# Two pairs of items in one stretch of 64x64 matmuls, masked scores in the place of k's columns

## The chip, the cores and the metric

The kernel runs on one core of one Trainium2 chip. The metric is the device time of one execution in microseconds (us), the median of several runs. The engines' names are those of the profile: PE (TensorE matmul), PEld (its weight loads), DVE (VectorE), ACT (ScalarE), POOL (GpSimd), SP (SyncE, which issues the DMAs).

## The reference

Retention (attention with a decay in place of the softmax) over 8 batches x 8 heads, sequence 576, head size 64, and behind it a feed-forward layer of 512 -> 2048 -> 512 on 4608 tokens, all in float32:

```python
scores = (q @ k.T) / sqrt(64)            # per batch and head
Dmat   = where(i >= j, gamma[h] ** (i - j), 0)
ret    = (scores * Dmat) @ v
x      = ret, heads side by side          # (4608, 512)
h      = x @ w_in                         # (4608, 2048)
out    = (h - tanh(h)) @ w_out            # (4608, 512)
```

## The kernel before, in words

The sequence is cut into 9 blocks of 64 positions (`C = 64`, `NC = 9`). A block holds 8 batches x 64 positions = 512 tokens (`BLK`). Retention goes block by block with a state per batch and head: a block's output is q times the state so far, plus the masked scores of the block itself times v; then k's rows times v are added to the state. An *item* is one batch in one block (8 heads, as 2 x 4 matrices of 64x64), a *pair* is two items; pair p belongs to block p // 4, and there are 36 (`NP`).

**Feed-forward.** Weights and x are split into a high and a low word, and three products are added. `mm1(n, f)` (L327) makes column block f of h for block n in 12 matmuls of 128x512 into one PSUM bank, `mm2(n, f)` (L393) multiplies the activated h of f by w_out in 12 matmuls into the four banks o0 to o3. Between them `activate` runs ACT tanh (L353), DVE subtraction (L354), ACT cast to the high word gh (L355), DVE subtraction to the low word gl (L356). `store` copies the four o banks at the end of a block (ACT L410, DVE L412) and stores them (L414).

**Retention.** All 64x64 matmuls have line L252 (`run`). `m_score` makes the scores of an item, `m_state` what is to be added to the state, `m_out` the output (`own`): first state times q, then v times masked scores. `run` lays two of the first list and two of the second side by side, so that the four quadrants of the array are used. `entry(p, sc)` is one *stretch*: scores of pair p + 1, states and outputs of pair p; behind it DVE masks the scores (L263, into the buffer pm), ACT and DVE split the output into xh and xl (L278, L280), and DVE adds to the state (L311). The trace shows each 64x64 matmul twice.

**PSUM has eight banks:** o0 to o3, two called h, one called new, one called own. mm1 takes the h banks in turn, and so do the scores of a stretch (`s`); the new states have `new` for themselves, and the outputs `own`.

**Order.** Every engine works its instructions in exactly the order in which the program writes them (`in_order`); semaphores are set by the framework from what reads and writes which tile.
- First part (`seq`, to about 125 us): block 0's items, then mm1 of blocks 0 and 1, while ACT and DVE convert the weights (`guard`, `unit`: L95 to L124). Results of mm1 that are needed later are spilled to DRAM.
- Second part (`late`, 32 steps k): mm2 of block 1 and then of block 0; spilled h are fetched (L363), activated (`resume`, `words`: L368 to L376). At k = 3, 8, 13 and 18 stands one stretch, for pairs 8 to 11.
- Third part: blocks n = 2 to 8. For each f: mm1(n, f), then mm2 of the f before. While block n is worked on, the items of block n + 1 get their retention: at f = 1, 5, 9 and 13 a stretch stands between mm1(n, f) and mm2(n, f - 1). Block 8 has none.

**Loads.** A pair's q, k (columns), v and k (rows) are one tile `a` of 1 MB, two buffers. Behind each stretch `load_pair(p + 2)` is issued on SP (L171) and POOL scales q and v (`prep`, L185, L186); the table for q changes with the block (L161).

Of the kernel before, what the change touches and what calls it, by code (L numbers as in the profile page):

```python
# [9 lines left out]
F32 = mybir.dt.float32  # L10
# [12 lines left out]
C = 64  # L23
# [8 lines left out]
WARM = 26  # L32

# [34 lines left out]
def retention_ffn(ctx: ExitStack, tc: tile.TileContext, ins, out, spill):  # L68
# [10 lines left out]


# [10 lines left out]
    def guard(t, f, begin=False):  # L91

        if (t, f) not in masks:
            masks[t, f] = pool.tile([P, DM], I32, tag="cv", bufs=3, name=f"m{t}{f}")
            nc.scalar.activation(masks[t, f], wraw[t, f][:, :, 1].bitcast(F32), AF.Tanh, scale=STEP)  # L95
            if begin:
                return
# [32 lines left out]
    last, going, pace = [], [], []  # L130
# [22 lines left out]
    loaded, scored, xs, qtabs = {}, {}, {}, {}  # L153
# [9 lines left out]
    def load_pair(p, u=None):  # L163

        if p >= NP:
            return
        c, pr = divmod(p, B // 2)
        load_qtab(c)
        a = loaded["pair", p] if u == 1 else pool.tile([P, 2, 4, 4, C], F32, tag="a", name=f"a{p}")
        if u is None:  # L170
            nc.sync.dma_start(a, qkv_d[c - 1, 2 * pr : 2 * pr + 2].rearrange("u p t i s -> p u t i s"))  # L171
        else:
            nc.sync.dma_start(a[:, u], qkv_d[c - 1, 2 * pr + u])
        loaded[2 * p], loaded[2 * p + 1] = a[:, 0], a[:, 1]
        loaded["pair", p] = a
        loaded["qv", p] = a[:, :, 0], a[:, :, 2]

    def prep(p, q=True):
# [3 lines left out]
        a = loaded["pair", p]  # L182
        if q:
            table = qtabs[c].unsqueeze(1).broadcast_to([P, 2, 4, C])
            nc.gpsimd.tensor_tensor(a[:, :, 0], a[:, :, 0], table, op=ALU.mult)  # L185
        nc.gpsimd.tensor_tensor(  # L186
            a[:, :, 2], a[:, :, 2], vtab[:, c].unsqueeze(1).unsqueeze(3).broadcast_to([P, 2, 4, D]), op=ALU.mult
        )
# [3 lines left out]
    def load_early(p):  # L192
        c, pr = divmod(p, B // 2)
        if pr < 2:
            return load_pair(p)
        src = qkv_d[c - 1, 2 * pr : 2 * pr + 2].rearrange("u p t i s -> p u t i s")
        parts = []
        for t in range(2):
            parts.append(const.tile([P, 2, 2, 4, C], F32, tag=f"wo{2 * (pr - 2) + t}", name=f"a_early{p}_{t}"))
            nc.sync.dma_start(parts[t], src[:, :, 2 * t : 2 * t + 2])  # L200
            behind(tc, pace[-1])
        for u in range(2):
            loaded[2 * p + u] = Parts([part[:, u] for part in parts])
        loaded["qv", p] = parts[0][:, :, 0], parts[1][:, :, 0]

    def scale_q(p):
        q, table = loaded["qv", p][0], qtabs[p // (B // 2)]
        nc.vector.tensor_tensor(q, q, table.unsqueeze(1).broadcast_to([P, 2, 4, C]), op=ALU.mult)

    def scale_v(p):  # L210
        v = loaded["qv", p][1]
# [43 lines left out]
    def after_score(j, sc, n):  # L255
# [5 lines left out]
        else:  # L261
            pm = pool.tile([P, 2, 4, C], F32, tag="pm", bufs=1, name=f"pm{j}")
            nc.vector.tensor_tensor(  # L263
                pm[:, :n].rearrange("p u i q -> p (u i) q"), sc.rearrange("p u i q -> p (u i) q"),
                mask.unsqueeze(1).broadcast_to([P, 4 * n, C]), op=ALU.mult,
# [22 lines left out]

    def entry(p, sc, more=None):
        c0, pr = divmod(p, B // 2)  # L290
        new = psp.tile([P, 2, 4, D], F32, tag="new", bufs=1, name=f"new{p}")
        o = psp.tile([P, 2, 4, C], F32, tag="own", bufs=1, name=f"own{p}")
        same, other = [], []
        for u in range(2):
            if p + 1 < NP:
                same += m_score(2 * p + 2 + u, sc[:, u])
            other += m_out(2 * p + u, o[:, u])
        if c0 < NC - 1:
            for u in range(2):
                same += m_state(2 * p + u, new[:, u])  # L300
# [3 lines left out]
        if p + 1 < NP:  # L304
            after_score(2 * p + 2, sc, 2)
# [3 lines left out]
        if c0 < NC - 1:  # L309
            st = state[:, 2 * pr : 2 * pr + 2]  # L310
            nc.vector.tensor_tensor(st, new, st, op=ALU.add)  # L311
# [342 lines left out]
```

## Time and profile before

| | |
|---|---|
| median of 3 runs | 890.01 us (889.89 to 890.73) |
| profiled execution | 891.8 us, span 890.0 us, mean granted PE clock 0.995 |
| PE busy | 877.6 us, 99% of the span |
| PEld / DVE / ACT / POOL busy | 724.3 / 363.3 / 287.7 / 67.7 us |
| 64x64 matmuls and their weight loads | L252 |
| stretches from block 2's items on | 28 |

A row of the timeline gives start and duration in us, engine, line, operation, output <- inputs, shape, and in brackets how long the engine stood idle before it and what released it. Rows of the chain are start, duration and what ran. A matmul's end is modelled, so PE's pace is read from the spacing of the starts. In a table by windows stand for each stretch of time the busy us of PE, PEld, DVE, ACT and POOL, then the granted PE clock, the share of the DMA engines and GB/s.

### The profile page before, as it was taken

The page shows a single profiled execution, that of the slowest core. Times are in us where ns is not written, and L with a number is a line of the kernel's source. Part 1 is how long each engine was busy: PE and PEld are TensorE (multiplying, and loading weights), DVE is VectorE, ACT ScalarE, POOL GpSimd, SP SyncE. Part 2 cuts the span into 40 slices and gives each one's busy share as a digit, 9 for nine tenths or more (in the row PEclk, how much of TensorE's full clock was granted, in tenths as well). Part 3 has the DMA queues.
Part 4 walks back from the last instruction along what each step waited for, and adds up shares of the span by engine and source line. Part 5 has one row for each costly group of instructions (what it writes and reads, how often), then busy time and mean ns, then how long its engine had stood idle before and what let it go on. Part 6 is the DMA issues. An engine that isn't in the chain of part 4 may idle for free.

```text
span 890.0 us, 17595 instructions
## 1 busy us (share of the span) xinstructions
PE 877.6 (99%) x7848; PEld 724.3 (81%) x7848; DVE 363.3 (41%) x548; ACT 287.7 (32%) x503; POOL 67.7 (8%) x59
## 2 busy tenths in 40 slices
PE   7999999999999999999999999999999999999997
PEld 6777878788888888888888888888888888888886
DVE  6879777653432332333233233323323322222222
ACT  4887774443222222222222222222222221222222
POOL 0001001210111110111111111111000111000000
PEclk8999999999999999999999999999999999999999
DMA  9966965551311131102111131113111201002001
GB/s 354 325 231 212 342 193 171 167 167 48 96 54 49 48 96 49 54 30 68 47 54 49 49 95 54 49 48 96 49 54 47 62 35 48 1 1 49 1 1 47
DMA packets 31372, 82.06 MB, mean 92 GB/s; under 512 B 3776, under 2 KB 4928, under 8 KB 31296
## 3 DMA queue, kind: packets, MB, share of 16 engines
q1 hardware_dynamic: 30768, 80.02, 27.8%
q8 instruction: 61, 1.00, 0.5%
q10 hardware_dynamic: 528, 0.92, 0.3%
q14 instruction: 15, 0.12, 0.0%
HBM read 63.62 MB, written 17.30 MB: 91 GB/s over the span
## 4 chain that ended last, share of the span: by engine, by line
PE 90%; DMA 3%; DVE 3%; ACT 2%; issue 0%; SPq 0%; DVEq 0%
PE o L393 44%; PE h L327 38%; PE s L252 3%; DMA rwo<-in_w_out_dram 2%; PE new L252 2%; PE own L252 2%; DMA rwi<-in_w_in_dram 1%; DVE mo L110 0%; DVE mo L112 0%; ACT mi L95 0%; ACT mi L98 0%; PE new_first L252 0%; DVE mi L105 0%; DVE wi L124 0%; ACT wi L117 0%
## 5 line engine op out<-in xcount | busy, mean ns | idle before, releaser
L327 PE MATMUL h<-xh,wi 128*128 128x512 f32 x1152 | 307.0, 392 | 2.7 <-ACT g L339 0.8
L393 PE MATMUL o<-wo,gh 128*128 128x512 f32 x1144 | 291.6, 393 | 0.4 <-DVE ob L412 0.4
L327 PEld LDWEIGHTS h<-xh,wi 128*128 128x128 f32 x1152 | 216.3, 189 | 49.7 <-ACT g L339 1.3
L393 PEld LDWEIGHTS o<-wo,gh 128*128 128x128 f32 x1144 | 212.3, 188 | 46.8 <-DVE ob L412 1.5
L354 DVE TENSOR_TENSOR g<-h,g 128x512 f32<-128x512 f32 x114 | 78.8, 691 | 367.1 <-ACT g L353 367.1
L353 ACT ACTIVATE g<-h 128x512 f32<-128x512 f32 x114 | 68.3, 599 | 420.9 <-PE h L327 420.1
L393 PE MATMUL o<-wo,gl 128*128 128x512 f32 x572 | 157.3, 389 | 0.0
L327 PE MATMUL h<-xl,wi 128*128 128x512 f32 x576 | 154.5, 390 | 0.0
L327 PEld LDWEIGHTS h<-xl,wi 128*128 128x128 f32 x576 | 108.7, 189 | 22.9
L393 PEld LDWEIGHTS o<-wo,gl 128*128 128x128 f32 x572 | 107.4, 188 | 22.3
L356 DVE TENSOR_TENSOR gl<-g,gh 128x512 fp32r<-128x512 f32 x113 | 81.0, 717 | 77.5 <-ACT gh L355 70.0
L355 ACT CAST gh<-g 128x512 fp32r<-128x512 f32 x113 | 70.1, 620 | 86.2 <-DVE g L354 86.2
L185 POOL TENSOR_TENSOR a<-a,qtab 128x512 f32<-128x512 f32 x27 | 36.3, 1344 | 605.7 <-DMA a<-in_qkv_dram 547.3
L252 PE MATMUL own<-a,state 64*64 64x64 f32 x960 | 58.9, 221 | 0.0
L252 PE MATMUL own<-pm,a 64*64 64x64 f32 x960 | 57.5, 218 | 0.0
L252 PEld LDWEIGHTS own<-a,state 64*64 64x64 f32 x960 | 47.8, 134 | 0.4 <-issue 0.4
L252 PEld LDWEIGHTS own<-pm,a 64*64 64x64 f32 x960 | 48.0, 135 | 0.0
L252 PEld LDWEIGHTS s<-a 64*64 64x64 f32 x960 | 30.3, 134 | 10.6 <-issue 10.2
L186 POOL TENSOR_TENSOR a<-a,vtab 128x512 f32<-128x512 f32 x28 | 32.2, 1152 | 67.4 <-DVE mi L112 67.4
L252 PE MATMUL s<-a 64*64 64x64 f32 x960 | 34.4, 221 | 0.0
L376 DVE TENSOR_TENSOR gl<-s,gh 128x512 fp32r<-128x512 f32 x30 | 21.6, 720 | 31.2 <-PE o L393 24.4
L375 ACT CAST gh<-s 128x512 fp32r<-128x512 f32 x30 | 18.6, 621 | 39.0 <-PE o L393 27.4
(67 smaller groups left out, 465.0 us busy)
## 6 DMA issues: line engine op xcount, KB each, us to landing
a<-in_qkv_dram SPq DMA_DIRECT2D x29, 1024.0 KB, 5.2
out_dram<-ob SPq DMA_DIRECT2D x69, 128.0 KB, 2.4
rwi<-in_w_in_dram SPq DMA_DIRECT2D x16, 512.0 KB, 5.8
rwo<-in_w_out_dram SPq DMA_DIRECT2D x16, 512.0 KB, 5.1
s<-spill_dram SPq DMA_DIRECT2D x30, 256.0 KB, 2.7
spill_dram<-g SPq DMA_DIRECT2D x20, 256.0 KB, 5.2
a<-in_first_dram SPq DMA_DIRECT2D x7, 384.0 KB, 5.0
spill_dram<-home SPq DMA_DIRECT2D x10, 256.0 KB, 6.3
```

What stands on the lines that cost most here:

```text
L185: nc.gpsimd.tensor_tensor(a[:, :, 0], a[:, :, 0], table, op=ALU.mult)
L186: nc.gpsimd.tensor_tensor(a[:, :, 2], a[:, :, 2], vtab[:, c].unsqueeze(1).unsqueeze(3).broadcast_to([P, 2, 4, D]), op=ALU.mult)
L252: nc.tensor.matmul(out_, w, x, start=start, stop=stop)
L327: nc.tensor.matmul(hp, win[f][:, a, cc, :], x[:, cc, :], start=(k == 0), stop=(k == 3 * NCC - 1))
L353: nc.scalar.activation(g, h, AF.Tanh)
L354: nc.vector.tensor_tensor(g, h, g, op=ALU.subtract)
L355: nc.scalar.copy(gh, g)
L356: nc.vector.tensor_tensor(gl, g, gh.bitcast(F32), op=ALU.subtract)
L375: nc.scalar.copy(gh, g)
L376: nc.vector.tensor_tensor(gl, g, gh.bitcast(F32), op=ALU.subtract)
L393: nc.tensor.matmul(ops[n][t], g[:, t * P : (t + 1) * P], wout[f_][:, a, :], start=(f_ == first and k == 0), stop=(f_ == final and k == 2),)
```

## The change

From pair 8 on, two stretches become one of two *halves*. `entry2(p)` does pairs p and p + 1: first half scores of p + 1, states and outputs of p; then, with no full-size matmul between, states of p + 1, scores of p + 2, outputs of p + 1. The states no longer have the bank `new`: scores and states of both halves take the two h banks in turn, and the second half's outputs go into `new`.

```diff
+    def entry2(p):
+        more, states = p + 2 < NP, p // (B // 2) < NC - 1
+        sc, o = bank(f"s{p + 1}", "h"), bank(f"own{p}", "own")
+        same = pair(m_score, p + 1, sc)
+        if states:
+            new = bank(f"new{p}", "h")
+            same += pair(m_state, p, new)
+        run(same, pair(m_out, p, o))
+        for u in range(2):
+            after_score(2 * p + 2 + u, sc[:, u : u + 1], 1)
+        if states:
+            add_state(p, new)
+        low = after_out(2 * p, o, 2, False)
+        o, same = bank(f"own{p + 1}", "new"), []
+        if states:
+            new = bank(f"new{p + 1}", "h")
+            same += pair(m_state, p + 1, new)
+        if more:
+            sc = bank(f"s{p + 2}", "h")
+            same += pair(m_score, p + 2, sc)
+        run(same, pair(m_out, p + 1, o))
+        if states:
+            add_state(p + 1, new)
+        low()
+        if more:
+            after_score(2 * p + 4, sc, 2)
+        after_out(2 * p + 2, o, 2)
+        for q, t in ((p + 2, 1), (p + 3, 1), (p + 3, 0), (p + 4, 0)):
+            load_part(q, t)
+            prep(q, t)
...
+    def add_state(p, new):
+        st = state[:, 2 * (p % (B // 2)) : 2 * (p % (B // 2)) + 2]
+        nc.vector.tensor_tensor(st, new, st, op=ALU.add)
```

The stretches stand at other places: in the second part at k = 4 and 14, in blocks 2 to 7 at f = 3 and 11 and behind mm2, so that mm1 of the next f follows.

```diff
-        if k in (3, 8, 13, 18):
-            entry(p, psp.tile([P, 2, 4, C], F32, tag="h", bufs=2, name=f"s{n}_{f}"))
-            p += 1
+        if k in (4, 14):
+            entry2(p)
+            p += 2
...
             mm1(n, f)
-            if n + 1 < NC and f % 4 == 1:
-
-                sc = psp.tile([P, 2, 4, C], F32, tag="h", bufs=2, name=f"s{n}_{f}")
-                entry((n + 1) * B // 2 + f // 4, sc)
             todo.append((n, f))
             if (n, f) != (NC - 1, NF - 2):
                 mm2(*todo.pop(0))
+            if n + 1 < NC and f in (3, 11):
+
+                entry2((n + 1) * B // 2 + f // 8 * 2)
```

A pair is loaded as two tiles of 512 KB, `qk` (q and k's columns, three buffers) and `vr` (v and k's rows, two), and pm is gone: the masked scores are written over k's columns.

```diff
-            pm = pool.tile([P, 2, 4, C], F32, tag="pm", bufs=1, name=f"pm{j}")
+            u = j % 2
+            pm = parts[j // 2, 0][:, u : u + n, 1]
...
+        if k == 18:
+            load_part(B + 2, 0)
```

The small buffers of the first two parts (masks of the weights, spilled h, tanh, output copies) get places with fixed numbers instead of two rings: for the output copies

```diff
-            ob = pool.tile([P, DM], F32, tag="cv", bufs=3, name=f"ob{n}_{t}")
+            ob = place(2 + t % 3, f"ob{n}_{t}")
```

How the order on the engines changes, at three places. *First, the stretch in block 6.* PE, the end of a stretch before (`a` is the pair, `new` the states, `own` the output, `o_0` and `o_1` the banks of mm2):

```order
L252 MATMUL new_6014<-a_5661 64x64 x2
L252 MATMUL own_6015<-a_5661,state 64x64 x2
L252 MATMUL new_6014<-a_5661 64x64 x2
L252 MATMUL own_6015<-pm_5860,a_5661 64x64 x2
L393 MATMUL o_0_6091<-wo_1214,gh_0_5959 128x512 [waits Activation_49]
L393 MATMUL o_1_6092<-wo_1214,gh_0_5959 128x512 [waits DVE_49]
```

PE now, the end of a merged stretch (`qk` and `vr` are the pair's two tiles):

```order
L265 MATMUL s_6194<-qk_5840 64x64 x2
L265 MATMUL own_6192<-qk_5837,state 64x64 x2
L265 MATMUL s_6194<-qk_5840 64x64 x2
L265 MATMUL own_6192<-qk_5837,vr_5834 64x64 x2
L368 MATMUL h_4_6278<-xh_5343,wi_432 128x512 [waits DVE_49]
L368 MATMUL h_4_6278<-xh_5343,wi_432 128x512 x3
```

Instead of mm2, mm1 follows (`h_4`), in the h bank that held the second half's states, and it waits for DVE. On DVE, the work of a stretch before:

```order
L354 TENSOR_TENSOR g_1_6006<-h_1_5993,g_1_6006 128x512 [waits Activation_49]
L356 TENSOR_TENSOR gl_1_6008<-g_1_6006,gh_1_6007 128x512 [waits Activation_49]
L263 TENSOR_TENSOR pm_6080<-s_1_6013,mask 128x512 [waits PE_49]
L280 TENSOR_TENSOR xl_6083<-own_6015,xh_6082 128x2x4x64 [waits Activation_49]
L311 TENSOR_TENSOR state<-new_6014,state 128x512
L354 TENSOR_TENSOR g_2_6120<-h_2_6107,g_2_6120 128x512 [waits Activation_49]
```

DVE now, for a merged stretch:

```order
L400 TENSOR_TENSOR gl_3_6102<-g_3_6100,gh_3_6101 128x512 [waits PE_49,Activation_49]
L278 TENSOR_TENSOR qk_5837<-s_6119,mask 128x256 [waits DMAHW3_49,PE_49,Pool_49]
L278 TENSOR_TENSOR qk_5837<-s_6119,mask 128x256
L308 TENSOR_TENSOR state<-new_6121,state 128x512 [waits PE_49]
L308 TENSOR_TENSOR state<-new_6193,state 128x512 [waits PE_49]
L295 TENSOR_TENSOR xl_6190<-own_6120,xh_6189 128x2x4x64 [waits Activation_49]
L278 TENSOR_TENSOR qk_5840<-s_6194,mask 128x2x256 [waits DMAHW4_49,PE_49,Pool_49]
L294 TENSOR_TENSOR xl_6190<-own_6192,xh_6189 128x2x4x64 [waits Activation_49]
```

The first masks are two pieces with one wait between them, for the last of the scores; each state addition has a wait of its own for PE. *Second, DVE at the first stretch of the second part.* Before (k = 3; `mo` and `wo` are a weight being converted, gl_2, s_3 and s_4 the h that are activated):

```order
L376 TENSOR_TENSOR gl_2_1681<-s_2_1605,gh_2_1680 128x512 [waits PE_49,Activation_49]
L369 TENSOR_TENSOR s_3_1636<-s_3_1636,th_3_1684 128x512 [waits DMAHW1_49,Activation_49]
L124 TENSOR_TENSOR wo_1666<-mo_1609,wo_1666 128x512 [waits DVE_49]
L263 TENSOR_TENSOR pm_1757<-s_1_1690,mask 128x512 [waits PE_49]
L280 TENSOR_TENSOR xl_1760<-own_1692,xh_1759 128x2x4x64 [waits Activation_49]
```

And now (k = 4):

```order
L420 TENSOR_TENSOR gl_2_1677<-s_2_1602,gh_2_1676 128x512 [waits PE_49,Activation_49]
L413 TENSOR_TENSOR s_3_1632<-s_3_1632,th_3_1680 128x512 [waits DMAHW5_49,Activation_49]
L137 TENSOR_TENSOR wo_1662<-spare,wo_1662 128x512 [waits DVE_49]
L420 TENSOR_TENSOR gl_3_1699<-s_3_1632,gh_3_1698 128x512 [waits PE_49,Activation_49]
L413 TENSOR_TENSOR s_4_1658<-s_4_1658,th_4_1702 128x512 [waits DMAHW6_49,Activation_49]
L278 TENSOR_TENSOR qk_1162<-s_1707,mask 128x256 [waits PE_49]
L278 TENSOR_TENSOR qk_1162<-s_1707,mask 128x256
```

Two more operations stand ahead of the masks. *Third, PE at the start of a block.* Before, mm1(6, 1) and behind it the stretch:

```order
L327 MATMUL h_1_5993<-xl_5243,wi_350 128x512 x4
L327 MATMUL h_1_5993<-xh_5242,wi_350 128x512 x4
L252 MATMUL s_1_6013<-a_5865 64x64 [waits DMAHW4_49,DVE_49,Pool_49]
L252 MATMUL s_1_6013<-a_5865 64x64
L252 MATMUL own_6015<-a_5661,state 64x64 [waits PE_49]
```

And now, mm1(6, 1) and behind it mm2(6, 0):

```order
L368 MATMUL h_1_6019<-xh_5343,wi_354 128x512 x4
L437 MATMUL o_0_6039<-wo_1216,gh_0_5985 128x512 [waits Activation_49]
L437 MATMUL o_1_6040<-wo_1216,gh_0_5985 128x512 [waits DVE_49]
L437 MATMUL o_2_6041<-wo_1216,gh_0_5985 128x512 [waits Activation_49]
L437 MATMUL o_3_6042<-wo_1216,gh_0_5985 128x512 [waits DVE_49]
```

The four output copies of the block before, which these waits are for, no longer have a stretch's time.

More of the change, by code (lines that the diff above doesn't have):

```diff
@@ L32 @@
 WARM = 26
+LATE = 22
 NP = NC * B // 2
@@ L93, in guard @@
         if (t, f) not in masks:
[L94 removed]
+            k = stream.index((t, f))
+            if k < LATE:
+                masks[t, f] = place(k % 3, f"m{t}{f}", I32)
+            else:
+                if not spare:
+                    spare.append(pool.tile([P, 4, DM], I32, tag="xl", name="spare"))
+                masks[t, f] = spare[0][:, k % 4]
             nc.scalar.activation(masks[t, f], wraw[t, f][:, :, 1].bitcast(F32), AF.Tanh, scale=STEP)
@@ L167, in load_pair, with prep @@
         c, pr = divmod(p, B // 2)
[L168 to L178, printed above, removed]
+        if t == 0:
+            load_qtab(c)
+        if (p, t) not in parts:
+            tag = ("qk", "vr")[t]
+            parts[p, t] = pool.tile([P, 2, 2, 4, C], F32, tag=tag, bufs=3 - t, name=f"{tag}{p}")
+            for u in range(2):
+                loaded.setdefault(2 * p + u, Parts([None, None])).parts[t] = parts[p, t][:, u]
+        src = qkv_d[c - 1, 2 * pr : 2 * pr + 2].rearrange("u p t i s -> p u t i s")
+        queue.dma_start(parts[p, t][:, at], src[:, at, 2 * t : 2 * t + 2])
+    def load_pair(p):
+        for t in range(2):
+            load_part(p, t)
+    def prep(p, t):
         if p >= NP:
@@ L287, in first_states, with bank, pair @@
         return ms, lambda: nc.scalar.copy(state[:, b : b + 2], new)
-    def entry(p, sc, more=None):
[L290 to L300, printed above, removed]
+    def bank(name, tag):
+        return psp.tile([P, 2, 4, D], F32, tag=tag, bufs=2 if tag == "h" else 1, name=name)
+    def add_state(p, new):
+        st = state[:, 2 * (p % (B // 2)) : 2 * (p % (B // 2)) + 2]
+        nc.vector.tensor_tensor(st, new, st, op=ALU.add)
+    def pair(what, p, bank):
+        return what(2 * p, bank[:, 0]) + what(2 * p + 1, bank[:, 1])
+    def entry(p, sc, more=None):
+        new, o = bank(f"new{p}", "new"), bank(f"own{p}", "own")
+        same, other = pair(m_score, p + 1, sc) + pair(m_state, p, new), pair(m_out, p, o)
         if more is not None:
```

72 lines of the change are left out of this document (34 added, 38 removed).

## The prediction

> **What bounds the kernel now.** I read the page first (busy times, then the chain that ended last), then the chain in order of time, then one 64x64 stretch on the timeline, and then the four places at which the change sets a new neighbour beside TensorE.
>
> ```profile
> PE 877.6 (99%) x7848; PEld 724.3 (81%) x7848; DVE 363.3 (41%) x548; ACT 287.7 (32%) x503; POOL 67.7 (8%) x59
> PE 90%; DMA 3%; DVE 3%; ACT 2%; issue 0%; SPq 0%; DVEq 0%
> ```
>
> PE is the bound: 99% of the span, 90% of the chain. What PE does not have to wait for costs nothing; every wait that is added to it is added to the time. VectorE is at 41%, so its work is cheap, but its *lateness* at one place is not.
>
> ```profile
> 493.23 2.95 PE o L393 x12
> 496.18 2.72 PE h L327 x12
> 517.24 2.95 PE o L393 x12
> ```
>
> The chain gives the size of a block's pieces: 12 full matmuls are 2.72 us (0.2267 each), and one stretch comes every 517.24 - 493.23 = 24.01 us. Eight pieces of 2.72 are 21.76, so a stretch costs 24.01 - 21.76 = 2.25 us in all. The same stretch on the timeline:
>
> ```profile
> 503.27 1.07 PE L327 MATMUL h<-xh,wi 128*128 128x512 f32 x4
> 506.38 0.69 DVE L356 TENSOR_TENSOR gl<-g,gh 128x512 fp32r<-128x512 f32 x1 [0.69 <-ACT gh L355]
> 514.15 1.07 PE L327 MATMUL h<-xh,wi 128*128 128x512 f32 x4
> 515.15 0.27 PE L252 MATMUL s<-a 64*64 64x64 f32 x2
> 516.07 0.23 PE L252 MATMUL s<-a 64*64 64x64 f32 x2
> 516.13 0.22 PE L252 MATMUL new<-a 64*64 64x64 f32 x2
> 517.02 0.23 PE L252 MATMUL own<-pm,a 64*64 64x64 f32 x2
> 517.17 2.11 PE L393 MATMUL o<-wo,gh 128*128 128x512 f32 x8
> 517.33 0.58 ACT L278 CAST xh<-own 128x512 fp32r<-128x512 f32 x1
> 518.07 0.68 DVE L263 TENSOR_TENSOR pm<-s,mask 128x512 f32<-128x512 f32 x1
> 518.67 0.68 DVE L280 TENSOR_TENSOR xl<-own,xh 128x512 fp32r<-128x512 f32 x1
> ```
>
> The stretch runs from t0 = 515.15 to E = 517.05 (one spacing after its last matmul). The scores are issued by t0 + 0.93, and the other 16 groups follow at 0.058 us each. Its 32 groups of four are 32 x 0.0585 = 1.87 us. The remaining 2.25 - 1.87 = 0.38 us is the price of going from 128x128 to 64x64 and back. One more number: the engine that reads the last product (issued 517.03) starts at 517.33, so a result reaches the next engine 0.30 us after its matmul's issue. The last two rows show VectorE's operations of 0.68 us starting 0.60 apart when nothing holds them.
>
> **The change, part by part.**
>
> *Merging.* 28 stretches become 14, so 14 prices of 0.38 go: 14 x 0.38 = **-5.3 us** (-4.6 to -6.0 at 0.33 to 0.43). The matmuls themselves stay the same in number.
>
> *The wait behind the stretch.* Until now mm2 (into the o banks) followed, and the state addition had 2.7 us of cover. Now mm1 of the next f follows at once, into the h bank that held the second pair's new states. That bank is free only when the state addition has read it, and the addition may not write the state before the last own product has read it. That product stands in the last step but one, issued at E - 0.13. The prices:
>
> ```profile
> L311 DVE TENSOR_TENSOR state<-new,state 128x512 f32<-128x512 f32 x28 | 19.1, 682 | 0.0
> L260 DVE TENSOR_TENSOR pm<-s_first,decay 128x256 f32<-128x256 f32 x8 | 3.4, 423 | 6.5 <-PE s_first L252 6.0 <-PE own_first L252 0.3
> ```
>
> VectorE starts at E - 0.13 + 0.30 = E + 0.17, ends 0.68 later at E + 0.85, and PE goes on about 0.06 later (the hand-over 803.46 + 0.69 to 804.21 below): E + 0.91, where mm2 started at E + 0.12. That is 0.80 us, at the 10 merged stretches of blocks n = 2 to 6 (n = 7 has no states, the two late ones are followed by mm2): **+8.0 us** (0.68 to 0.95 each: +6.8 to +9.5). A gain is excluded, because PE stands still here. Late behind it are only the low word of x and the next masks, which have two 2.72 us pieces before anyone needs them.
>
> *The wait in the middle.* The second half's first state products go into the bank of the scores that must have been masked, in two 128x256 pieces. Both wait for the last score: start t0 + 0.93 + 0.30 = t0 + 1.23. Pieces behind each other start 0.35 apart (0.42 less the 0.08 by which the 0.68 us operations overlap), so the second ends at t0 + 2.00 and PE goes on at t0 + 2.06, where it would have at t0 + 1.91. With the first weights loading unhidden I take 0.20 us x 10. VectorE is free in time because the stretch now comes behind mm2: the row at 506.38 shows gl over at 507.07, 2.9 us behind mm1's last issue, and mm2 takes 2.72. In block 7 only the second step needs the masks (2 x 0.05), and at the second late stretch two VectorE operations stand ahead (0.3). Together **+2.4 us** (+0.7 to +5). The bank for the following scores is free earlier: addition at t0 + 2.15 to 2.83, wanted at t0 + 3.0. That costs nothing as long as the middle is late too.
>
> *The first late stretch* (k = 4, where VectorE still converts weights):
>
> ```profile
> 132.00 1.08 PE L393 MATMUL o<-wo,gl 128*128 128x512 f32 x4
> 132.48 0.62 ACT L375 CAST gh<-s 128x512 fp32r<-128x512 f32 x1
> 138.43 0.62 ACT L375 CAST gh<-s 128x512 fp32r<-128x512 f32 x1 [0.41 <-DVE s L369]
> 138.96 0.63 ACT L368 ACTIVATE th<-s 128x512 f32<-128x512 f32 x1
> 137.04 0.69 DVE L376 TENSOR_TENSOR gl<-s,gh 128x512 fp32r<-128x512 f32 x1 [1.21 <-ACT gh L375]
> 138.25 0.69 DVE L124 TENSOR_TENSOR wo<-mo,wo 128x512 fp32r<-128x512 f32 x1
> 138.86 0.69 DVE L263 TENSOR_TENSOR pm<-s,mask 128x512 f32<-128x512 f32 x1
> ```
>
> In the program before, PE left this stretch at 135.03 and VectorE masked its scores at 138.86, 3.8 us later, with nobody waiting. Now PE does wait. VectorE's list up to 138.25 is the same; then come gl (its cast ends at 139.05) at 139.09, s at 139.69, the masks at 140.30 and 140.65 to 141.07; PE at 141.13. PE itself: its next mm2 waits for the cast of 132.48 (ends 133.10; 0.39 us that the old stretch hid), runs 2.72, and its stretch would be in the middle at 138.0. 0.39 + 3.1 = **+3.5 us** (+2 if the earlier part leaves VectorE less behind, +5 if more).
>
> *The start of a block.* The old stretch at f = 1 stood between mm1 and mm2(n, 0); the new ones at f = 3 and 11 do not. mm2(n, 0) needs the bank that the fourth output copy empties, and that copy waits for the store of the first, whose buffer it takes. Block 8 has no stretch and shows the bare case, block 5 the covered one:
>
> ```profile
> 803.46 0.69 DVE L412 COPY ob<-o 128x512 f32<-128x512 f32 x1 [2.20 <-PE h L327]
> 803.20 0.84 PE L393 MATMUL o<-wo,gh 128*128 128x512 f32 x3
> 804.21 1.45 PE L393 MATMUL o<-wo,gh 128*128 128x512 f32 x5 [0.16 <-DVE ob L412]
> 806.41 1.08 PE L327 MATMUL h<-xh,wi 128*128 128x512 f32 x4
> 419.28 0.69 DVE L412 COPY ob<-o 128x512 f32<-128x512 f32 x1 [2.22 <-PE h L327]
> 421.12 2.11 PE L393 MATMUL o<-wo,gh 128*128 128x512 f32 x8
> ```
>
> Without the wait 806.41 would be 803.20 + 2.72 = 805.92: 0.49 us. After the change the first and fourth output still share one place, so blocks 2 to 7 pay it: 6 x 0.49 = **+2.9 us** (+1.0 by the marked 0.16 alone, +3.6 at 0.6).
>
> *Loads.* After the first late stretch three halves of pairs, a table and a fourth half are queued on SP ahead of the next spill fetch, and the table waits for the scaling of the third half.
>
> ```profile
> SPq L161 <- POOL a L185: 34.2, 5, 7.6
> 138.18 0.39 SPq L171 DMA_DIRECT2D a<-in_qkv_dram  x1
> 143.36 1.77 POOL L185 TENSOR_TENSOR a<-a,qtab 128x512 f32<-128x512 f32 x1 [56.87 <-DMA a<-in_qkv_dram]
> ```
>
> Such a load lands 5.2 us after its issue and its scaling takes 1.4 to 1.8, so the fetch leaves some 8 us behind the stretch and is used, over three operations, some 14 us behind it, when mm2 asks for it. I take **+0.3 us** (0 to +4). In the blocks these loads have 40 us. Masks in the place of k's columns cost nothing: the scores that read k are over when the mask starts, and no other engine reads k's columns later. The smaller tiles for masks, spills and outputs keep the depth that they had; I take 0 for the part before 125 us (-1 to +1, from the longest wait that a copy there costs PE):
>
> ```profile
> 113.52 1.20 PE L327 MATMUL h<-xh,wi 128*128 128x512 f32 x4 [0.85 <-ACT g L339]
> ```
>
> *The clock.* The late stretch holds PE idle for 3.1 us. The start of the trace shows what idling does:
>
> ```profile
> 6.00:7.00 1.00, 0.22 (x6) 0.22 (x8) 0.36 (x1) 0.00 (x0) 0.00 (x0) 1.00 1.03 423
> 13.05 0.27 PE L252 MATMUL s_first<-a 64*64 64x64 f32 x2 [1.44 <-DMA a<-in_first_dram]
> 14.00:15.00 1.00, 0.98 (x45) 1.00 (x47) 0.86 (x3) 0.40 (x2) 0.00 (x0) 0.89 1.07 414
> 15.00:16.00 1.00, 1.00 (x22) 0.98 (x22) 1.00 (x3) 0.95 (x3) 0.00 (x0) 0.50 0.95 385
> 21.00:22.00 1.00, 1.00 (x5) 0.82 (x4) 0.96 (x2) 0.00 (x0) 0.00 (x0) 0.69 1.05 391
> ```
>
> (The column before the DMA share is the granted clock.) About 0.9 us idle around 6 to 7 left it at 1.00, so the 0.8 us waits should too. 1.44 us and some smaller gaps were followed by 0.50 from 14.9 to 21.7 us, 6.8 us at half speed, 3.4 us lost. I take half of that, since dense work follows the late stretch, for one time: **+1.7 us** (0 to +3.4).
>
> [...]
>
> **Sum.** -5.3 + 8.0 + 2.4 + 3.5 + 2.9 + 0.3 + 1.7 = +13.5 us. The profiled execution has a span of 890.0 us and took 891.8; the median of the runs shown is 890.01, so against that median: 890.0 + 13.5 = **903.5 us**.
>
> **The rivals.**
>
> *The hand-overs are covered* (faster). The mechanism is the merge alone: VectorE releases each bank before PE wants it, as it does at every stretch of the program before. Then only -5.3 is left: 884.7. For it speaks VectorE's 41%; against it that two of the four waits are for products that PE has only just issued, the third for a list of VectorE's that ends at 141 us, and that the fourth stands in block 8's rows. It decides where all waits together stay under 5.3 us, 0.38 per merged stretch; the wait behind the stretch alone is put at twice that.
>
> *The clock stays.* Everything else as above: 890.0 + 11.8 = 901.8. For it: one 3.1 us gap between dense stretches is not the ragged start. Against: the row at 13.05.
>
> *Waits half as long*, because releases come earlier than I lined up: 8.0 + 2.4 + 3.5 + 2.9 = 16.8 becomes 8.4, and less the 5.3 it is 893.1, or 890 to 897. For it: the 0.30 us from issue to next engine was read at one place. Against: the state addition's own 0.68 us cannot shrink.
>
> *The queue.* The spill fetch is late by 4 us rather than 0.3: 907 to 911.
>
> **How the numbers follow.** Forecast with the lost clock 0.46; the clock stays 0.30; waits half as long 0.10; hand-overs covered 0.08; queue 0.06. All terms at their low ends give 894.5, at their high ends 915.9; not all will stand at one end, so the range is 897 to 909, which takes in the first two cases and part of the queue's. Within 0.2% (1.8 us, about what three runs of this kernel can tell from no change) is a slice of the half-length case: 0.03. Faster 0.08, slower 0.89.
>
> **What would show it.** In the profile after: ten waits of PE (or its weight loads) for the state addition, 0.8 to 0.9 us each; PE held for the masks around 138 to 141 us; six waits for the output copy at block starts; a period of 48.0 - 0.38 + 1.0 us per merged stretch; a granted clock below 1.00 at 140 to 148 us. I am wrong if mm1 behind a merged stretch starts within 0.2 us of its end, or if the first late stretch's masks run before 139 us.

## The result, and the profile after

The changed kernel takes **921.42 us** (919.35 to 925.92, four executions) against 889.95 us for the kernel before on the same chip: ratio 1.0361, 95% interval 1.0320 to 1.0403. Slower, as forecast, but by 31.5 us and not by 13.5; it lies above the range of 897 to 909. The profiled execution took 925.92 us with a span of 924.1, that is 34.1 more than the span before. (Times below are medians too; of e9's four executions one took 1777.47 us and is left out.)

The page of the changed kernel, first the busy times, then the queue that brings instructions (packets, MB, share of the DMA engines), then the chain that ended last:

```profile
PE 887.0 (96%) x7847; PEld 731.1 (79%) x7848; DVE 366.6 (40%) x562; ACT 288.2 (31%) x503; POOL 68.8 (7%) x59
...
q8 instruction: 61, 1.00, 0.5%
...
PE 83%; DMA 5%; DVE 4%; ACT 4%; issue 3%; ACTq 0%; SPq 0%; DVEq 0%
```

PE is now 96% busy, and a name stands in the chain that had 0% before: "issue", time in which PE waits for nothing that the profile shows. PE's waits, in total, times and longest (the kernel before has no row with `own`, `new` or the state in it):

```profile
PE own L265 <- issue: 8.0, 7, 2.0
PE h L368 <- DVE state L308: 6.8, 10, 0.7
PE new L265 <- issue: 4.9, 3, 2.9
PE s L265 <- issue: 3.3, 3, 1.1
PE o L437 <- DVE ob L456: 1.9, 7, 0.4
PE o L437 <- ACT gh L419: 0.7, 1, 0.7
```

The second, fifth and sixth row are the waits that the prediction priced. The other three, 16.2 us, lie *inside* the merged stretches; 2.9 of it is the forecast wait for the masks in the first late one, and the rest was not forecast. (By the starts of the matmuls, without modelled ends, the unforeseen gaps are twelve with 15.6 us.) One of them on the timeline, the same block 6 as in the prediction (start, duration, engine and line; in brackets the idle time before and what ended it):

```profile
501.95 0.27 PE L265 MATMUL s<-qk 64*64 64x64 f32 x2
...
503.82 0.23 PE L265 MATMUL own<-qk,vr 64*64 64x64 f32 x2
504.06 0.27 PE L265 MATMUL new<-vr 64*64 64x64 f32 x2
...
505.70 0.23 PE L265 MATMUL own<-qk,vr 64*64 64x64 f32 x2
507.04 0.27 PE L265 MATMUL s<-qk 64*64 64x64 f32 x2 [1.12 <-issue]
507.28 0.23 PE L265 MATMUL own<-qk,vr 64*64 64x64 f32 x2
...
508.20 1.45 PE L368 MATMUL h<-xh,wi 128*128 128x512 f32 x4 [0.70 <-DVE state L308]
509.45 1.91 PE L368 MATMUL h<-xl,wi 128*128 128x512 f32 x4
511.16 1.65 PE L368 MATMUL h<-xh,wi 128*128 128x512 f32 x4
...
507.45 0.69 DVE L308 TENSOR_TENSOR state<-new,state 128x512 f32<-128x512 f32 x1 [2.68 <-PE own L265]
```

Matmuls are counted here as the trace counts them, 256 in a merged stretch. Four things stand in these rows. Between 503.82 and 504.06 lies the middle wait for the masks, 0.2 us longer than the usual spacing. Between 505.70 and 507.04 PE stands for 1.3 us between matmul 240 and 241 of 256, 16 before the end; nothing of the program ends then. From 507.28 to 508.20 it waits for the state addition of 507.45, as forecast. And mm1 then takes 508.20 to 512.64 in place of 2.72 us: the granted clock is 0.50 from 508.95 to 512.36. Windows of 3.41 us show which idling came before such a drop (the number ahead of the DMA share is the granted clock):

```profile
136.90:140.31 3.41, 0.63 (x41) 0.66 (x45) 3.13 (x6) 1.62 (x3) 0.00 (x0) 1.00 0.49 148
140.31:143.72 3.41, 3.41 (x103) 3.19 (x94) 1.00 (x2) 0.59 (x1) 1.04 (x1) 0.50 0.47 164
...
505.54:508.95 3.41, 1.59 (x46) 1.24 (x38) 1.50 (x3) 0.59 (x1) 0.29 (x1) 1.00 0.57 158
508.95:512.36 3.41, 3.41 (x9) 2.65 (x9) 0.99 (x2) 0.00 (x0) 1.19 (x2) 0.50 0.77 225
...
607.94:611.35 3.41, 1.89 (x37) 1.44 (x29) 1.85 (x4) 0.59 (x1) 0.14 (x1) 1.00 0.54 172
611.35:614.76 3.41, 3.41 (x17) 2.81 (x16) 1.33 (x3) 0.64 (x2) 1.65 (x2) 1.00 0.80 240
```

After a window with 0.63 or 1.59 us busy (18% and 47%) comes one at 0.50; after 1.89 us (55%) none. This execution has four such drops behind 100 us (at 140, 304, 407 and 509 us), 1.7 us of work each.

### The profile page after: what moved, and what is told of

It reads as the page before. It is cut to its first block, busy times and chain, and to the rows that moved or that the text cites. A ratio compares the mean times of both kernels' runs of the same rounds, so it can differ in the third digit from the quotient of the medians.

```text
span 924.1 us, 17829 instructions
## 1 busy us (share of the span) xinstructions
PE 887.0 (96%) x7847; PEld 731.1 (79%) x7848; DVE 366.6 (40%) x562; ACT 288.2 (31%) x503; POOL 68.8 (7%) x59
## 4 chain that ended last, share of the span: by engine, by line
PE 83%; DMA 5%; DVE 4%; ACT 4%; issue 3%; ACTq 0%; SPq 0%; DVEq 0%
PE o L437 40%; PE h L368 36%; PE s L265 3%; PE new L265 2%; PE own L265 2%; DMA out_dram<-ob 2%; DMA rwo<-in_w_out_dram 1%; DMA a<-in_first_dram 1%; DVE state L308 1%; ACT ob L454 1%; DMA spill_dram<-home 1%; DVE ob L456 1%; DVE g L398 1%; ACT g L397 0%; DVE mo L125 0%
## 5 line engine op out<-in xcount | busy, mean ns | idle before, releaser
L204 POOL TENSOR_TENSOR vr<-vr,vtab 128x512 f32<-128x512 f32 x28 | 30.2, 1079 | 639.9 <-DMA vr<-in_qkv_dram 559.3
L265 PE MATMUL own<-qk,state 64*64 64x64 f32 x960 | 61.4, 224 | 5.0 <-issue 5.0
L265 PE MATMUL own<-qk,vr 64*64 64x64 f32 x960 | 60.0, 221 | 3.0 <-issue 3.0
L265 PEld LDWEIGHTS own<-qk,state 64*64 64x64 f32 x960 | 49.5, 136 | 5.5 <-issue 5.5
L265 PEld LDWEIGHTS own<-qk,vr 64*64 64x64 f32 x960 | 49.7, 137 | 3.4 <-issue 3.4
L204 POOL TENSOR_TENSOR qk<-qk,qtab 128x512 f32<-128x512 f32 x27 | 38.4, 1424 | 58.5 <-DMA qk<-in_qkv_dram 44.3
L292 ACT CAST xh<-own 128x512 fp32r<-128x512 f32 x32 | 18.7, 585 | 75.0 <-PE own L265 75.0
L265 PEld LDWEIGHTS s<-qk 64*64 64x64 f32 x960 | 32.1, 137 | 9.7 <-issue 9.0
L265 PE MATMUL s<-qk 64*64 64x64 f32 x960 | 36.4, 224 | 3.3 <-issue 3.3
L265 PE MATMUL new<-vr 64*64 64x64 f32 x832 | 30.7, 221 | 5.2 <-issue 4.9
```

The costliest lines, as they stand in the source:

```text
L204: nc.gpsimd.tensor_tensor(a, a, table, op=ALU.mult)
L265: nc.tensor.matmul(out_, w, x, start=start, stop=stop)
L292: nc.scalar.copy(xh, o)
```

## The experiments: what the idle time inside a stretch is

Theory **S** (supply): the instructions themselves come late. The queue row above has 61 packets with 1.00 MB, 16 KB each, and PE with PEld has 15,695 instructions: some 257 to a packet, 128 weight loads and 128 matmuls. A merged stretch of 256 matmuls crosses two edges of such pieces. In the stretch shown they lie at matmul 112 (503.6 us) and 240; the packet for the piece behind the second edge starts at 504.36, takes 1.29, and PE goes on at 507.04, 3.4 us after the first edge, while the 128 matmuls between last only 2.1. The packet records speak for S at all twelve gaps: PE goes on 1.27 to 1.54 us after the end of such a packet, whatever the matmul. Rival **H**: a hand-over that the trace does not name.

**e1: move the edges, not the work.** Forty more matmul records at the very start.

```diff
-    busy(WARM, P)
+    busy(WARM + 40, 50)
```

> The changed kernel with 66 warm-up matmuls of 50 columns in place of 26 of 128 at the very start: 40 more matmul records ahead of everything, about the same warm-up time, nothing else moved. Theory S (supply): TensorE takes its instructions in pieces of 16 KB, 256 instructions, so 128 weight loads with their 128 matmuls; a merged stretch of 256 matmuls crosses into a new piece twice, 128 apart, and uses up a piece in some 2.1 us, before the one after it is there. Then the idle place inside each stretch moves 40 matmuls earlier: from matmul 229, 184, 246, 181, 243, 178, 240, 175, 237, 172, 234 to about 189, 144, 206, 141, 203, 138, 200, 135, 197, 132, 194, each still 0.8 to 2.2 us. Rival H (a hand-over that the trace doesn't name: a bank, a mask, a store): it belongs to the work and stays at the same matmuls. Both: the 0.2 us at matmul 128 stays, the time stays at 919 to 926.

918.29 us in one execution. The idle places moved to matmul 189, 206, 203, 200, 197 and 194 of their stretches, exactly 40 earlier, with 0.6 to 1.3 us. The timeline at that place in block 6, the stretch that starts at 499.63:

```profile
502.79 0.23 PE L265 MATMUL own<-qk,state 64*64 64x64 f32 x2
504.14 0.27 PE L265 MATMUL s<-qk 64*64 64x64 f32 x2 [1.12 <-issue]
```

H falls. But the five stretches whose second edge came to matmul 144 to 132 lost the idle time altogether, which S as I had it did not say. Their first edge lies at 16 to 4, and the packet for one of them started at 251.62 us, 1.1 us *ahead* of its stretch (252.75): here the next piece was asked for while wide matmuls still ran. The early part paid for the shift: two early stretches, beside the loading of weights, now met a second edge and stood for 1.1 and 4.5 us.

**e7: the supply by itself.** The kernel before, with a row of 64x64 matmuls on resident data behind the last mm2.

```diff
+    row(4)      # 12 wide matmuls, then 512 f32 64x64 matmuls over four quarters of the array
+    row(2)      # the same over two quarters
```

> The kernel before with extra work behind its last mm2: 512 f32 64x64 matmuls over four quarters of the array on resident data (1024 records, eight pieces), 12 wide ones ahead, then the same over two quarters only. Nothing waits for anything. Theory S: over four quarters the first two pieces go at 14.7 ns a record, then one piece of 128 records per 3.0 to 3.5 us, with an idle spot of 1.1 to 1.6 us every 128 records: 22 to 25 us for 1024 in place of 15.0. Over two quarters a record takes 29 ns, 3.75 us a piece, longer than a piece takes to come: 30 us, no idle spots over 0.3. Rival H: no idle spots in either, 15 and 30 us. The row adds about 58 us to the time.

The timeline at two of its stops, then 14 us windows, the first over four quarters and the second over two:

```profile
889.55 0.21 PE L606 MATMUL cross<-state 64*64 64x64 f32 x1 [1.24 <-issue]
...
893.04 0.21 PE L606 MATMUL cross<-state 64*64 64x64 f32 x1 [1.39 <-issue]
```

```profile
886.00:900.00 14.00, 8.58 (x535) 8.05 (x535) 0.00 (x0) 0.00 (x0) 0.00 (x0) 1.00 0.04 12
...
917.00:931.00 14.00, 14.00 (x487) 14.00 (x485) 0.00 (x0) 0.00 (x0) 0.00 (x0) 1.00 0.01 4
```

949.66 us in one execution. As S says, with nothing to wait for and idle DMAs, four quarters stop after every 128th record (151, 279, 407, ... 919), 1.4 to 2.1 us each, one piece per 3.5 to 4.0 us; 1024 records took 27.7 us, not 15.0 (S had put it at 22 to 25, a piece coming faster). Over two quarters, at 29 ns a record, PE is busy throughout: 30.0 us. At 14.7 ns a record, 1.88 us a piece, a 64x64 stretch over four quarters uses instructions 1.8 to 2.1 times as fast as they came here.

**e2, e3, e4: cut the stretch or move it.** The twelve matmuls of mm2 are set around the halves (h): in blocks 6, h, 6, h (e2); 6, h, h, 6 (e3); 4, h, 4, h, 4 (e4).

```diff
-                mm2(*todo.pop(0))
-                entry2(...)
+                pieces(entry2(...), (6, "h", 6, "h"), *todo.pop(0))    # e2
+                pieces(entry2(...), (6, "h", "h", 6), *todo.pop(0))    # e3
+                pieces(entry2(...), (4, "h", 4, "h", 4), *todo.pop(0)) # e4
```

> The merged stretch cut again into its two halves, with 6 of mm2's 12 matmuls ahead of the first half and 6 between the halves (12 between them in the two late ones); banks, tiles, places of f, order on DVE and ACT as in the changed kernel. Theory S: with 1.4 us of 128x512 matmuls between two crossings the next piece of instructions comes in time: the idle spots inside stretches (15.6 us with the late ones) go to under 1.5 us, the 0.2 us in the middle goes; the ten waits of mm1 for the state addition stay at 0.75 each more than before (7.5), the output copies at block starts stay (2.9), the late stretch costs 1 to 2, 14 more switches cost 5.3 and bring back the period of before. 890 + 7.5 + 2.9 + 1.5 = 902, range 900 to 905, clock 1.00 in the stretches after 20 us. Rival H: the idle stays inside the second half, 914 to 920. Rival C (the idle is the clock's doing): half clock and idle stay together.

> The merged stretch whole, but set in the middle of mm2 (6 matmuls ahead, 6 behind), so that 1.4 us of mm2 stand between the last state product and the next mm1. The ten waits for the state addition (0.75 each more than before) should go to 0.15 each: -7.5. Theory S: the idle inside the stretches stays, 1.0 to 1.3 each, 13 to 16 in all. Theory W (windows): the clock falls to a half for 3.41 us behind a window of that length in which TensorE was busy for less than about half; with 0.9 us less idle behind the same stall fewer windows get there, so 0 or 1 half-clock windows in the steady blocks in place of 3. 921.4 - 7.5 - 1.7 to -5 = 909 to 912. Rival (a stall always drops the clock): 913 to 915, with three or more half windows. If a bank is missed instead (the second bank of h is read later than I think), waits of 0.3 to 0.8 stand inside the first half and the time is 915 or more.

> mm2 in three pieces of 4: 4, first half, 4, second half, 4 (late ones: half, 6, half, 6): every hand-over of the merged stretch has 0.9 us of wide matmuls behind it. Theory S: no idle over 0.4 us inside stretches; the end waits fall from 0.9 to 0.2 or less; middle waits under 0.3. Left over before: block starts 2.9, late stretches 1 to 3, and up to 0.3 per stretch where a piece of instructions still comes late (crossings 1.88 + 0.37 + 0.91 = 3.2 us apart): 890 + 2.9 + 2 + 1 = 896, range 893 to 899. Rival H: 905 or more. It also bounds what tiles, masks in place and moved loads cost apart from the merge: all of 893 to 899 that isn't the block starts.

e2: 910.6 us, ratio 1.0235 (1.0212 to 1.0258). e3: 914.4, 1.0285 (1.0253 to 1.0317). e4: 908.3, 1.0204 (1.0186 to 1.0222). PE's waits from 200 to 900 us, e2 first, then e3, then e4:

```profile
PE h L379 <- DVE state L308: 6.9, 10, 0.7
PE o L448 <- DVE ob L467: 1.9, 7, 0.4
```

```profile
PE own L265 <- issue: 4.0, 5, 1.7
PE new L265 <- issue: 2.5, 3, 1.0
PE s L265 <- issue: 2.3, 3, 1.3
PE o L448 <- DVE ob L467: 1.9, 7, 0.4
PE new L265 <- PE own L265: 1.8, 10, 0.2
```

```profile
PE own L265 <- issue: 2.7, 1, 2.7
PE s L265 <- issue: 2.6, 1, 2.6
PE o L448 <- DVE ob L467: 2.0, 7, 0.4
PE new L265 <- issue: 0.3, 1, 0.3
```

Each wait answers to its own cause. Wide matmuls between the halves take the idle time away and leave the state addition (e2); wide matmuls behind the stretch take the addition away and leave the idle time (e3), and then no steady block loses its clock, though single gaps reach 1.9 us. All three lie above their ranges, however (by 5.6, 2.4 and 9.3 us), and two reasons show. In e4 two stretches stood for 2.75 and 2.94 us: the edge is at 295.7 us, SP issues a 512 KB load at 296.0, and the packet with the instructions starts only at 299.37, when the load's are through. The windows of e4 around it:

```profile
294.00:297.00 3.00, 3.00 (x136) 2.48 (x132) 2.31 (x5) 1.21 (x2) 0.00 (x0) 1.00 0.00 0
297.00:299.00 2.00, 2.00 (x123) 1.91 (x122) 0.05 (x1) 0.00 (x0) 0.00 (x0) 1.00 0.84 249
299.00:302.00 3.00, 0.44 (x8) 0.33 (x7) 1.29 (x2) 0.00 (x0) 1.04 (x1) 0.99 0.04 14
```

The DMA engines are 84% busy just while the packet is due; two halved windows followed. The second stretch has the same order: edge at 396.9, load from 397.2, packet at 400.64. That the load holds it up is the likely reading; no run moved that load alone. And in e2 the late part lost 4.3 us and then 3.4 us of clock to the fetch of a spilled block, the queue that the prediction gave 0.3 (in e4 the like wait is 3.0):

```profile
149.72 13.50 SPq L418 DMA_DIRECT2D s<-spill_dram  x6
...
154.47 0.63 ACT L423 ACTIVATE th<-s 128x512 f32<-128x512 f32 x1 [6.13 <-DMA s<-spill_dram]
...
156.58 3.78 PE L448 MATMUL o<-wo,gh 128*128 128x512 f32 x8 [4.34 <-ACT gh L430]
```

In the changed kernel, where the first late stretch is long, 0.7 us of it is left.

**e5, e6, e9: put the edges where they cost nothing.** With f = 8 in place of 11, both stretches of a block meet the edges at nearly the same matmul; e6 also sets them inside mm2 as e3 does (that edit is not shown again); e9 is e6 with 22 useless f32 matmuls (44 records) at k = 20 in place of more warm-up.

```diff
-            if n + 1 < NC and f in (3, 11):
+            if n + 1 < NC and f in (3, 8):
-    busy(WARM, P)
+    busy(WARM + 28, 61)          # e5 and e6 only
```

> The changed kernel with its second stretch of a block at f = 8 in place of 11, and 54 warm-up matmuls of 61 columns in place of 26 of 128. Between the stretches of a block now lie 5 x 24 + 256 = 376 matmuls, 8 less than three pieces of 128, so that both stretches of a block meet the pieces' edges at nearly the same place, and the warm-up sets that place: the first edge at matmul 28, 25, 22, 19, 16 of the f = 3 stretches and 20, 17, 14, 11, 8 of the f = 8 ones, the second 128 later. With the 40 matmuls of the shift before, stretches with the first edge at 4 to 16 had no idle spot. Theory S (supply; the sequencer runs ahead and asks for the next piece before the stretch begins): all ten steady stretches lose their 0.8 to 2.2 us, the late k=14 one keeps some at matmul 201; half-clock windows in the steady blocks go with them. Blocks of 98.0 instead of 99 to 102; 907, range 904 to 911, and up to 6 more if the early part, with weights loading, catches a late piece. Rival H: f = 3 to 8 changes nothing of it, 919 to 926.

> The aligned kernel with each steady stretch in the middle of mm2 as well (6 matmuls ahead, 6 behind), late ones as in the changed kernel. No idle at piece edges (theory S) and ten end waits of 0.15 in place of 0.9: 907 - 7.6, middle waits 0.37 in place of 0.2: +1.7. 901, range 898 to 905; left over against the time before are the late stretches (5 to 6), block starts (2.9), middle waits (3.7), less 14 switches (5.3). Rival H: 911 to 915 as with the stretch inside mm2 alone.

> Stretches at f = 3 and 8 in the middle of mm2 as in the last but one, the warm-up as in the changed kernel, and 22 f32 64x64 matmuls (44 records, about 1 us) of no use set at k = 20 of the first loop, behind the early stretches. So far a steady stretch had an idle spot where its first edge of a piece lay at matmul 22 or later, and none where it lay at 4 to 19. The 44 records put the first edges at about 12, 9, 6, 3, 0 (f = 3) and 18, 15, 12, 9, 6 (f = 8). Theory S: no idle spot over 0.15 us at an edge in any of the ten, where there were 8.3 us in all, and the early stretches keep theirs away as in the changed kernel. Waits at the end hidden, in the middle 0.37 each. 901, range 898 to 905. If an edge in the stretch always costs (the 4 to 19 were chance): 909 to 912.

e5: 921.4 us, 1.0361 (1.0344 to 1.0379). e6: 915.9, 1.0291 (1.0268 to 1.0315). e9: 905.3, 1.0171 (1.0146 to 1.0195), just above its range. The first two missed, by 14 and 15: only two of e5's ten stretches and none of e6's lost the idle time, and both paid 5 to 6 us in the early part. The edges lay elsewhere than I had counted, by 14 matmuls at f = 8 and by 6 at all of e6's (the mm2 matmuls ahead), and I had taken the limit too high. Put together, the ten steady stretches of five kernels (where no idle shows, the edge is counted on from its neighbours):

| first edge at matmul | stretches | idle at the second edge |
|---|---|---|
| 4 to 19 | e1: 16, 13, 10, 7, 4; e5: 19, 16; e9: 18, 15, 12, 9, 6 and 18, 15, 12 | none in any of 15 |
| 21 to 118 | after: all ten; e1: five; e5: eight; e6: ten; e9: 24, 21 | 0.46 to 2.2 us in every one of 35 |

The limit was sharp here: 19 is free, 21 costs 1.04 us. The packets differ likewise: in the 15 free stretches the one for the piece behind the second edge starts 0.40 to 3.12 us ahead of the stretch, in the 35 others 0.93 to 3.25 us behind its start. My estimate from the 19 and the 21 is that a piece is asked for some 20 matmuls (40 instructions) ahead of the array; no run shows it directly, and why the step is as large as from 0.40 ahead to 0.93 behind stays open. In e9 eight of ten stretches are free of it, and only the middle wait is left in them; the two others stand for 0.9 and 1.04 us. With a late wait of 2.2 us for a fetched block and one halved window (1.7) that is 5.8 us, more than the 4.3 by which it lies above its point. PE's waits of e9 from 200 to 900 us:

```profile
PE o L448 <- DVE ob L467: 1.9, 7, 0.4
PE new L265 <- PE own L265: 1.8, 10, 0.2
PE own L265 <- issue: 0.8, 1, 0.8
PE new L265 <- issue: 0.7, 1, 0.7
PE o L448 <- issue: 0.5, 1, 0.5
```

**e10, e11: what is left.** e10 is e9 with the late stretches in their four old places. e11 keeps everything of the change except the merge: the halves stand at f = 1, 5, 9 and 13, inside mm2.

> As the one before, with the two late stretches cut into their halves again, at k = 3, 8, 13 and 18 as in the kernel before the change; steady ones stay merged. It adds up what is left: 890 + 10 middle waits of 0.37 (3.7) + block starts 2.9 + the useless matmuls 1.0 - 10 merges at 0.38 (3.8) = 894, if the late part costs nothing once it is not merged. Rival Q (queue): the fetch of the spilled blocks waits on SP's queue behind loads as where the late stretches stood apart (4.8 us and a half clock of 3.4): 900 to 903. Point 896, range 893 to 903.

> Everything of the change but the merge: pairs as two tiles, masked scores in the place of k's columns, states and scores in h's two banks, the loads in their new order; the halves stand where the stretches of the kernel before stand (k = 3, 8, 13, 18 and f = 1, 5, 9, 13), in the middle of mm2. If the loss is the merge's alone (theory S with the waits that the trace names), the blocks have before's 96.05 to 96.3, the stretch at f = 1 hides the output copies again, and what is left is up to 1.9 us of one late wait for a fetched block: 890 to 892.5. Rival P (the parts cost something of their own: h's bank, masks in two pieces, loads behind others): blocks of 96.5 or more, 893 to 898.

e10: 899.3 us, 1.0116 (1.0097 to 1.0136). e11: 895.5, 1.0065 (1.0041 to 1.0089). e10's merged stretch without idle time and without end wait lasts 4.15 us and 0.37 for the switch, 4.52; two separate ones are 2 x 2.25 = 4.50. (Above its point are two stretches with an edge at 24 and 21, 2.2 us, a late wait of 1.7, and 1.6 us where the piece behind a free stretch came late: 5.5 of the profiled execution's 6.4; the median is 3.3 above.) The one block without any such stop takes 96.66 us, 0.6 more than the 96.05 before, as much as e11 shows for a block start. **Even then the merge gains nothing**: the middle wait of 0.37 eats the switch of 0.38. e11 has no idle in a stretch, inside a block its stretches follow at 24.01 to 24.05 us, and yet it is 6 us above the kernel before, and above the 890 to 892.5 for a loss that is the merge's alone. PE's waits say where some of that is:

```profile
PE o L438 <- DVE ob L457: 1.9, 7, 0.4
PE o L438 <- ACT gh L420: 1.2, 1, 1.2
```

Its blocks take 96.6 where 96.05 was the time before: the output copies still hold mm2(n, 0), since the stretch at f = 1 stands behind mm2's first six matmuls and not ahead of them (6 x 0.55 = 3.3 us), and one late wait for a fetched block costs 1.3. Rival P's numbers held, its reason only in part. The rest, 1.5 us in the medians, stays open.

**e8: the clock in the kernel before.** If a half-busy window costs clock, the one at 11.4 us in the kernel before (1.71 of 3.42 us busy) can be filled where PE waits for item 6.

```diff
-    busy(WARM, P)
+    busy(WARM - 5, 158)
+        if j == 3:
+            busy(5, BLK)
```

> The kernel before (not merged) with 5 more 512-column warm-up matmuls where TensorE waits 1.44 us for item 6 (11.6 to 13.05 us), and 5 fewer warm-up matmuls at the start of more columns (158 for 128), so that no matmul's number behind them changes. Theory W: the clock goes to a half behind a 3.41 us window in which TensorE is busy for less than about half; before, that is one window (0.50 busy from 11.37) and it costs 6.8 us at half clock, 3.4 us of work. Filled, no window is under 0.6 and the half clock goes: 886.5, range 885.5 to 888. Rival: the fill holds up item 6, or another early window falls under a half, and the time is 889 to 891.

890.12 us against 889.43, ratio 1.0003 (0.9991 to 1.0015): no gain. In the profiled execution the clock did stay at 1.00, where it had been halved (the same window of e8, then of the kernel before):

```profile
15.00:18.00 3.00, 2.27 (x47) 1.77 (x37) 2.92 (x8) 2.88 (x8) 0.00 (x0) 1.00 1.05 395
```

```profile
15.00:18.00 3.00, 2.41 (x27) 2.01 (x26) 2.60 (x7) 2.92 (x7) 0.00 (x0) 0.50 1.01 390
```

The rival's 889 to 891 came true, and the runs' clocks say why. Of the 15 executions of the kernel before in this comparison only four had a mean clock of 0.996, as an early half clock of 6.83 us leaves it, with a median of 891.0 us; the six at 0.999 or 1.000 had 889.2. The forecast took the profiled execution's loss for that of all. And e8's nine at 0.999 or 1.000 had 889.7, so the fill saves nothing where the clock was full already. No version tried beats the kernel before.

## Why the prediction was wrong, by its own steps

| step | forecast, us | profiled execution, us |
|---|---|---|
| merging, 14 x 0.38 | -5.3 | -5.3 (by e10's stretches) |
| wait behind the stretch | +8.0 | +7.5 (ten times 0.90 in place of 0.15) |
| wait in the middle | +2.4 | +2.3 (ten of 0.20 to 0.22, one of 0.33) |
| first late stretch | +3.5 | +3.1 |
| start of a block | +2.9 | +3.3 (six at 0.55, by e11's blocks) |
| spill fetch in the queue | +0.3 | +0.7 |
| clock | +1.7 | +6.8 (four halved windows of 3.41) |
| instruction supply | not in the sum | +15.6 (twelve gaps of 0.64 to 2.22) |
| early part | 0 | -1.4 (one halved window less than before) |

The sum of the right column is 32.6 of the 34.1; 1.5 is unassigned. In the other executions the mean clock was 0.995 and 0.996, not 0.990, so less was lost to halved windows; that goes with the lower median, +31.5.

**The step that failed first** is *Merging*. It said that the matmuls "stay the same in number" and took the price of the switch as all that joining two stretches does to PE. The measured half of it, 0.38 a switch, was right. Missing was what it does to the supply of instructions, 15.6 us: a stretch of 128 matmuls is about one piece, so one edge falls into it, while two fall into 256, and in the steady stretches PE stood at the second where the first lay at matmul 21 or later (35 of 35) and not where it lay at 4 to 19 (15 of 15). Why a piece does not come sooner, no run shows. (The kernel before has three early stretches of 160; no edge stopped them there, but e1's shift stopped two of them.) No row of the trace before showed such a wait; what it did show was the 61 packets on queue 8, and 1.00 MB over 15,700 instructions would have given the 128 matmuls. No rival had it either.

**The second** is *The clock*. I read single gaps (0.9 us idle had left it at 1.00, "so the 0.8 us waits should too"). What fits better is how busy a whole 3.41 us window is: the supply's 1.3 us and the addition's 0.9 us fall into one, 47% busy, and it drops (the four drops followed gaps of 3.1, 2.2, 1.2 and 1.3 us); e3, with the addition hidden, kept its clock in all ten steady stretches. The limit is not sharp: one window at 174.45 us, 45% busy, did not drop. Laid over the twelve traces with clock records, from 8 us on, the windows give 14 with at most 41% busy, each followed by half clock, and none so followed with 59% or more; between 45% and 56% seven were and twelve were not, so the share alone does not decide there.

**Right**: the waits behind and in the middle of the stretch, the first late stretch and the block starts, each within 0.5 us. The direction was no luck: with merging and the spill fetch these terms come to 11.6 us where 11.8 was said. Of "what would show it", the period per merged stretch failed: 507.8 us for ten, 50.8 each where 48.6 was said (supply 1.3, clock 0.5, block start 0.3), and the clock below 1.00 at 140 to 148 came as said but not only there. One of its two signs of being wrong showed too: the first late stretch's masks began at 138.83 us, before 139. It was a poor sign, since the stretch itself came 1.5 us earlier than lined up, and PE waited the 3.1 us all the same. One reading was off without effect: gl is over 3.1 us, not 2.9, behind mm1's last issue (503.95 in the trace before). Of the rivals, the queue's mechanism is real (e2, 4.3 us) but hidden here. "Waits half as long" and "hand-overs covered" are refuted by the ten waits of 0.7.

## What to carry to other kernels

Count instructions before you join small matmuls: in e7 TensorE got a piece of 128 matmuls with their weight loads per 3.5 to 4.0 us, so a stretch at 14.7 ns a matmul ran dry every 128 matmuls, for 1.4 to 2.1 us, and a 0.38 us switch now and then is cheaper than that. An "issue" wait that moves with unrelated instructions added ahead (in e1 by exactly the 40 matmuls) was supply here, not a hand-over; the packets of the instruction queue, which ended 1.27 to 1.54 us before PE went on, confirm it. Price a wait for the clock by how much of its 3.41 us window is left busy together with its neighbours, not by its own length (at 41% and less the clock was always lost here, at 59% and more never), and check that work moved away did not cover something else, like the output copies at f = 1.

## What the hardware showed that I had not expected

- Instructions came at a rate: with idle DMAs (e7) one 16 KB packet took 0.9 to 1.4 us, but PE went on only 3.3 to 4.0 us after the edge before, 1.4 to 1.6 of them after the packet's end.
- Instruction packets seem to queue behind data: beside 512 KB loads two of e4 started 3.7 and 3.8 us after their edges, where 0.5 to 0.8, once 1.5, stood in the changed kernel's steady stretches; beside the weights' loads, one of e1 started 4.0 us after its edge and the stretch stood for 4.5. No run shows it by itself.
- The half clock came in whole windows: its stretches lasted 3.41 or 6.83 us (the one that the end of an execution breaks off aside), and the times at full clock between them (122.88, 160.43, 98.99, 98.99 and 409.6 us in the changed kernel's clock records) are multiples of 3.413. A stall of much the same size dropped the clock in one block and not in another (1.24 us at 403.8 did, 1.35 us at 557.0 did not): the windows there were 49% and 55% busy.
